# Softmax rows turned on VectorE and put in place by GpSimd, and dense rows as 128 half rows, in a recurrent-memory transformer kernel

## The chip, the cores and the metric

The kernel runs on one core of a Trainium2 chip. The time is the device time of one execution in microseconds. A core has five engines that run their own instruction streams in order and wait for each other by semaphores: TensorE (PE; its weight loads are listed as PEld), VectorE (DVE), ScalarE (ACT), GpSimd (POOL) and SyncE (SP), which issues DMAs.

## The reference

Two layers, each an attention block with a recurrent memory followed by a dense block. The sequence of 2048 rows of 512 is cut into 64 segments of 32 rows; 8 memory rows stand ahead of each segment, and the attention's output for them is the memory of the next segment.

```python
for s in range(n_seg):
    xs = x[:, s * seg_len:(s + 1) * seg_len, :].copy()
    h = jnp.concatenate([mem, xs], axis=1)              # 40 rows
    q = jnp.einsum('btd,dhe->bhte', h, Wq)              # 32 heads of 128
    k = jnp.einsum('btd,dhe->bhte', h, Wk)
    v = jnp.einsum('btd,dhe->bhte', h, Wv)
    scores = jnp.einsum('bhqe,bhke->bhqk', q, k) * scale
    scores = jnp.where(mask[None, None], scores, -1000000000.0)
    p = _softmax(scores, axis=-1)
    o = jnp.einsum('bhqk,bhke->bhqe', p, v)
    o = jnp.einsum('bhte,hed->btd', o, Wo)
    mem = o[:, :M, :].copy()
    outs.append(o[:, M:, :])
...
x = x + _A_ref(_layernorm(x, axis=-1), A_mem0, A_Wq, A_Wk, A_Wv, A_Wo, A_seg_len)
x = x + _B_ref(_layernorm(x, axis=-1), B_w1, B_w2)      # relu(x w1) w2, inner size 1376
x = x + _A_ref(_layernorm(x, axis=-1), ...)
x = x + _B_ref(_layernorm(x, axis=-1), B_w1, B_w2)
```

## The kernel before

The two layers run interleaved: step k works on segment k of the first layer and segment k - 2 of the second, so there are 66 steps, and 62 of them have both. The 40 rows of each layer stand side by side as 80 columns of a transposed tile `HT` (two of them take turns). All weights stay in SBUF.

A step has these parts. `queries_keys` multiplies the weights of four heads with `HT` (16 matmuls of 80 columns) and copies the result from PSUM to `qT` or `kT`. `scores` does one *unit*: the list `UNITS` has three whole units of eight heads and two half units of four. A unit's scores land in one PSUM bank; VectorE adds the mask (L1144), takes the maximum (L1148), subtracts it (L1151); ScalarE takes the exponential (L1155); VectorE sums (L1158), inverts (L1161) and multiplies into the bf16 tile `P` (L1175; GpSimd can do that too). Then TensorE turns `P` with an identity (L726, `work<-ident,P`), and two masked evictions bring the turned rows to `PT`, once for each half of the partitions, so that the other half is zero (L1198 on ScalarE, L1200 on VectorE). `attend` multiplies values by `PT` (L1217) into `OT`, and `project` multiplies `OT` by `Wo` into the bank `st`. Its memory columns go to the next step's `HT`, its other columns to `OX`.

`finish` is the rest of the layers: `OX` is turned by a DMA to `y` (L920), added to `x` (L924), and `dense_layer` normalises the 64 rows (32 of each layer), turns them (`fill<-ident,xr`), multiplies by `w1` and `w2` (L821). The total goes to `Z` (tile `vx`, L940). The first layer's 32 rows of it are normalised again and turned into the next `HT` as the second layer's input; the statistics go through `rstd`, whose two small operations run on GpSimd (L731, L736). GpSimd also narrows the finished rows for the store (L962), carries the first layer's result into `x` (L957), widens the new input rows (L909) and copies rows to `HT` (L998). Values for later segments are made ahead of time in `late_values` and pass through DRAM.

The order on every engine is made while the kernel is built. Each operation is recorded by `plan.op` with the engines it may run on, planned costs, and what it reads and writes. TensorE's operations are sorted by the table `PLACE` (places in a step, one for each operation and phase); the others follow from planned start times, from `AHEAD` and from the window `LOOK`. So a change of an operation moves the order on all engines, and each engine then runs its list strictly in order. `PAIRED` names the groups that run as pairs of half-width matmuls. Tiles come from rings: `es` (the softmax rows in f32) has two buffers, `PT` three, the PSUM `work` ring five banks.

Of the kernel before, what the change touches and what calls it, by code (L numbers as in the profile page):

```python
# [30 lines left out]
LOOK = 0.0763052  # L31
PERIOD = 26.155362
PLACE = {
# [187 lines left out]
def t_dve(n, rate=1):  # L221
    return 0.07 + 1.042e-3 * n / rate


PART, MASKED = {ACT: 0.13, DVE: 0.10}, {ACT: 0.11, DVE: 0.065}
XBAR = 0.5, 0.2, 2.6


# [1147 lines left out]
```

## Time and profile before

| | |
|---|---|
| runs | 1592.23, 1590.45, 1588.74 us; median 1590.45 |
| profiled execution, first to last instruction | 1588.6 us |
| TensorE busy | 1569.5 us, 99% |
| ScalarE busy | 1165.2 us, 73% |
| VectorE busy | 1082.3 us, 68% |
| GpSimd busy | 314.3 us, 20% |
| granted TensorE clock | 0.998 |

The times do not say which of the runs was profiled; the span is 0.14 us under the fastest and 1.85 us under the median. Matmuls are pipelined, and their ends are modelled in the profile: a group's start and the next group's start tell what it occupies. A line such as L726 or L984 is that of a helper with many callers, so the tiles' names tell the groups apart.

### The profile page before, as it was taken

Reading aid. Unit: us, or ns where it says so; the run is one execution under the profiler, and the core shown is the slowest. Engines: PE = TensorE matmul, PEld = TensorE weight load, DVE = VectorE, ACT = ScalarE, POOL = GpSimd, SP = SyncE. Lnnn points to the kernel's source line nnn. Section 1 sums busy time; section 2 is a strip of 40 time slices with the busy share of each in tenths; the row PEclk is TensorE's granted clock in tenths of the full one; section 3 lists DMA queues with packets and bytes.
Section 4 is the critical chain, followed back from the end, with each engine's and each line's share of the span. In section 5 each row is a group of like instructions: output and inputs, shape, how many; then the busy total and the mean of one; then the engine's idle time right before and its main releaser. Section 6 shows DMA issues by size and latency. Waiting matters only on the chain.

```text
span 1588.6 us, 100346 instructions
## 1 busy us (share of the span) xinstructions
PE 1569.5 (99%) x45458; PEld 1411.1 (89%) x45458; DVE 1082.3 (68%) x2957; ACT 1165.2 (73%) x3073; POOL 314.3 (20%) x667
## 2 busy tenths in 40 slices
PE   8999999999999999999999999999999999999998
PEld 5689999999999989999989999999998998898887
DVE  4566766766776776686676677677667667667665
ACT  4667777777777777777777777777777777777774
POOL 5112112212112212121121221211211121112110
PEclk9999999999999999999999999999999999999999
DMA  9711111111111111111111111111111111111100
GB/s 371 243 44 30 26 33 32 29 35 37 25 39 31 35 29 33 29 32 40 26 36 27 35 26 42 37 26 38 25 35 28 33 33 29 33 25 22 28 21 9
DMA packets 76540, 70.89 MB, mean 45 GB/s; under 512 B 50920, under 2 KB 62416, under 8 KB 76112
## 3 DMA queue, kind: packets, MB, share of 16 engines
q1 hardware_dynamic: 70096, 44.14, 13.1%
q0 software_dynamic: 4992, 19.40, 3.4%
q8 instruction: 356, 5.83, 1.6%
q10 hardware_dynamic: 1024, 0.93, 0.2%
q14 instruction: 72, 0.59, 0.1%
HBM read 31.53 MB, written 9.96 MB: 26 GB/s over the span
## 4 chain that ended last, share of the span: by engine, by line
PE 97%; DMA 1%; DVE 1%; POOL 1%; ACT 0%; issue 0%; DVEq 0%; POOLq 0%
PE work L726 40%; PE st L726 19%; PE fill L1048 16%; PE fill L726 8%; PE fill L821 5%; PE work L1217 5%; PE work L1133 4%; DMA xg<-in_A_x_dram 0%; DMA y<-OX 0%; DMA w_sb<-in_B_w_dram 0%; ACT HT L982 0%; POOL Wo_sb L537 0%; PE fill L711 0%; DVE ln L749 0%; POOL ln L736 0%
## 5 line engine op out<-in xcount | busy, mean ns | idle before, releaser
L726 PE MATMUL work<-HT,Wq_sb 128*128 128x80 bf16 (+2 forms) x10400 | 361.8, 201 | 3.1 <-ACT HT L982 3.1
L726 PE MATMUL work<-HT,Wk_sb 128*128 128x80 bf16 (+2 forms) x10416 | 362.7, 201 | 0.8 <-ACT HT L982 0.8
L726 PEld LDWEIGHTS <-Wq_sb 128*128 128x128 bf16 (+1 forms) x10400 | 330.9, 104 | 20.8 <-issue 6.0
L726 PE MATMUL st<-OT,Wo_sb 128*128 128x80 bf16 (+1 forms) x8448 | 345.5, 201 | 0.0
L726 PEld LDWEIGHTS <-Wk_sb 128*128 128x128 bf16 (+1 forms) x10416 | 327.1, 104 | 17.3 <-issue 2.0
L726 PEld LDWEIGHTS <-Wo_sb 128*128 128x128 bf16 x8448 | 315.7, 100 | 13.0 <-issue 12.7
L1048 PE MATMUL fill<-Wv_sb,HT 128*64 128x512 bf16 x2112 | 273.6, 381 | 1.1 <-DVE HT L984 1.0
L982 ACT CAST kT<-work 128x320 bf16<-128x320 f32 (+1 forms) x523 | 218.3, 418 | 68.6 <-PE work L726 31.1
L982 ACT CAST qT<-work 128x320 bf16<-128x320 f32 (+1 forms) x516 | 215.7, 418 | 67.5 <-PE work L726 47.2
L1198 ACT ACTIVATE PT<-work,half 128x160 bf16<-128x160 f32 (+1 forms) x515 | 231.3, 463 | 20.1 <-PE work L726 12.7
L982 ACT CAST OT<-work 128x320 bf16<-128x320 f32 (+1 forms) x461 | 186.2, 420 | 50.7 <-PE work L1217 50.6
L982 ACT CAST vw<-fill 128x512 bf16<-128x512 f32 x229 | 134.1, 586 | 113.3 <-PE fill L1048 109.8
L1144 DVE TENSOR_TENSOR es<-work,maskb 128x320 f32<-128x320 f32 (+2 forms) x330 | 136.2, 413 | 99.7 <-PE work L1133 93.2
L924 DVE TENSOR_TENSOR xg<-xg,y 64x512 f32<-64x512 f32 x65 | 44.2, 680 | 227.2 <-DMA y<-OX 226.6
L731 POOL TENSOR_SCALAR ln<-ln 32x1 f32<-32x1 f32 (+2 forms) x159 | 46.6, 293 | 566.7 <-DVE ln L752 561.0
L1155 ACT ACTIVATE es<-es 128x320 f32<-128x320 f32 (+2 forms) x330 | 136.1, 413 | 24.4 <-DVE es L1151 16.2
L1048 PEld LDWEIGHTS <-HT 128*64 128x64 bf16 x2112 | 98.9, 110 | 57.0 <-DVE HT L984 1.2
L1151 DVE TENSOR_TENSOR es<-es,mx 128x320 f32<-128x320 f32 (+2 forms) x330 | 136.3, 413 | 4.9
L1148 DVE TENSOR_REDUCE mx<-es 128x8 f32<-128x320 f32 (+2 forms) x330 | 133.9, 406 | 5.4
L1158 DVE TENSOR_REDUCE sm<-es 128x8 f32<-128x320 f32 (+2 forms) x330 | 133.4, 404 | 5.1 <-ACT es L1155 2.2
L1175 DVE TENSOR_TENSOR P<-es,sm 128x320 bf16<-128x320 f32 (+1 forms) x269 | 126.9, 472 | 3.3
L1133 PEld LDWEIGHTS <-qT 128*40 128x40 bf16 x4096 | 93.3, 97 | 35.6 <-ACT qT L982 13.6
(96 smaller groups left out, 2164.8 us busy)
## 6 DMA issues: line engine op xcount, KB each, us to landing
V<-vw SPq DMA_DIRECT2D x248, 48.0 KB
V<-vh SPq DMA_DIRECT2D x120, 64.0 KB
Wq_sb<-in_A_Wq_dram POOLq DMA_DIRECT2D x2, 2048.0 KB, 23.2
Wk_sb<-in_A_Wk_dram POOLq DMA_DIRECT2D x2, 2048.0 KB, 28.6
Wo_sb<-in_A_Wo_dram POOLq DMA_DIRECT2D x2, 2048.0 KB, 39.4
vh<-vg SPq DMA_DIRECT2D x32, 128.0 KB
xb<-in_A_x_dram SPq DMA_DIRECT2D x16, 128.0 KB
Wv_sb<-in_A_Wv_dram POOLq DMA_DIRECT2D x1, 2048.0 KB, 13.2
```

Of the source, the lines that this page charges most:

```text
L726: nc.tensor.matmul(out_[u:v, :], lhsT=lhsT[:, u:v], rhs=rhs, start=start, stop=stop, tile_position=(0, u), **more)
L821: nc.tensor.matmul(yp[64 * u:64 * u + 64, 0:256], lhsT=hT[:, fc, :], rhs=w2_sb[:, fc, 256 * u:256 * u + 256], start=(fc == 0), stop=(fc == ...
L982: nc.scalar.copy(out=out_, in_=in_)
L1048: nc.tensor.matmul(vp[64 * b:64 * b + 64, :], lhsT=cols(c4), rhs=Wv_sb[:, c4, n * 512:(n + 1) * 512], start=(c4 == 0), stop=(c4 == NC4 - 1 ...
L1133: nc.tensor.matmul(v[64 * g2:64 * g2 + L, a, i, b, :], lhsT=qT[:, hi, a * L:(a + 1) * L], rhs=kT[:, hi, a * L:(a + 1) * L], start=True, st ...
L1144: nc.vector.tensor_tensor(out=flat(es[:, A]), in0=flat(sp[:, A]), op=ALU.add, in1=maskb[:, a_lo:a_hi, :].unsqueeze(2).to_broadcast([128, n ...
L1148: nc.vector.tensor_reduce(out=mx[:, As], in_=es3(), axis=AX.X, op=ALU.max)
L1151: nc.vector.tensor_tensor(out=es3(), in0=es3(), op=ALU.subtract, in1=mx[:, As].unsqueeze(2).to_broadcast([128, ns * na, L]))
L1155: nc.scalar.activation(out=es[:, A], in_=es[:, A], func=ACTF.Exp, scale=SCALE)
L1158: nc.vector.tensor_reduce(out=sm[:, As], in_=es3(), axis=AX.X, op=ALU.add)
L1175: (nc.gpsimd if eng == POOL else nc.vector).tensor_tensor(out=o, in0=flat(es[:, A]), op=ALU.mult, in1=sm[:, As].rearrange("p (a s) -> p a ...
L1198: nc.scalar.activation(out=o, in_=i, func=ACTF.Copy, scale=half[:, b:b + 1])
```

## The change

The softmax rows are no longer turned by TensorE. The two heads of a pair now lie in neighbouring bf16 elements, so that a pair is one 32-bit element; the two groups of partitions hold the heads of the two halves of a unit. One VectorE transpose of 32x32 blocks of such elements a unit writes to the unit's `es` buffer. As each block is turned in its place only, the blocks are then copied to `PT`: two copies (`stay`) of the blocks that remain on their partitions and four (`shift`) of those that change them, planned on GpSimd or VectorE. `PT` is zeroed once and has 64 columns a pair with gaps; the attention matmuls read every second bf16 of it. `es` has three buffers.

The dense rows become 128 rows of 256: row 64u + t holds two of the four 128-column blocks of row t. The statistics of two halves are swapped across partitions by two small copies and joined by the aggregate. The turns take two matmuls in place of four, the store two DMAs in place of one, and widen and carry two copies in place of one.

Some tiles move into others' space (`ob` and `xe` into `vx`, `none` and `mb0` into `P`). `PLACE`, `PAIRED`, `AHEAD` and `LOOK` have new numbers. By the built program, 1024 turns of 80 columns leave TensorE, 330 block transposes enter VectorE, and of the 1980 copies 1416 stand on GpSimd and 564 on VectorE.

```diff
-LOOK = 0.0763052
+LOOK = 0.08909153
...
-    p_es = ring("es", 2, [128, 8 * L], F32)
-    p_PT = ring("PT", 3, [128, 2, 4, 2, L])
+    p_es = ring("es", 3, [128, 8 * L], F32)
+    p_PT = ring("PT", 3, [128, 4, 2, 128])
...
+    def layernorm_halves(x, keys, quick=False):
...
+        def swap(eng):
+            for u in range(2):
+                copy_on(eng, ln[64 * u:64 * u + 64, 8:14], ln[64 - 64 * u:128 - 64 * u, 0:6])
...
+        plan.op(DVE, t_dve(256), stats, r=keys, w=[ln])
+        plan.op((ACT, DVE), (0.2, 0.2), swap, w=[ln])
+        plan.op(DVE, 0.11, aggr, w=[ln])
+        rstd(ln, R, quick)
+        plan.op(DVE, 0.26, norm, r=[ln, *keys], w=[xn])
...
-        xnT, xn = p_xm.buf(), layernorm(x, keys, slice(0, n), last)
-        turned(xn, n, ident[:, 0:n], [(NC4 * n, lambda: xnT[:, :, :], same, [], [xnT])])
+        xnT, xn = p_xm.buf(), layernorm_halves(x, keys, last)
+        turned(xn, n, ident[:, :], [(NC4 * n, lambda: xnT[:, :, :], same, [], [xnT])], 2)
...
             def carry():
-                nc.gpsimd.tensor_copy(out=x[R1, :], in_=Z[R0, :])
+                for u in range(2):
+                    nc.gpsimd.tensor_copy(out=x[64 * u + SEG:64 * u + 64, :], in_=Z[64 * u:64 * u + SEG, :])
...
         def block():
-            nc.vector.tensor_tensor(out=flat(es[:, A]), in0=flat(sp[:, A]), op=ALU.add,
-                                    in1=maskb[:, a_lo:a_hi, :].unsqueeze(2).to_broadcast([128, na, ns, L]))
+            nc.vector.tensor_tensor(out=ekg(), in0=sp[:, A].rearrange("p (j g k) -> p j k g", k=L, g=2), op=ALU.add,
+                                    in1=maskb[:, mine, :].unsqueeze(3).to_broadcast([128, nx * na, L, 2]))
...
-        plan.op(DVE, t_dve(n), sub, r=[mx], w=[es])
+        plan.op((POOL, DVE), (t_pool(n), t_dve(n)), sub, r=[mx], w=[es])
...
+        pieces = [(a, a + 1) for a in range(a_lo, a_hi)] if nx == 2 else [(a_lo, a_hi)]
...
-        plan.op(PE, nx * na * 0.0358, turn, r=[*[("P", p, b, x) for b in range(2) for x in xs], "ident"], w=[tp, PT],
-                tile=EITHER, count=nx * na)
...
-            copy_op(n, keep, r=[tp, PT, "half"], w=[(PT, b)], more=MASKED)
+        def turn():
+            nc.vector.transpose(out=es[:, 0:64 * nj].rearrange("p (j k) -> p j k", k=64),
+                                in_=P[:, 0:512].bitcast(F32).rearrange("p (j k) -> p j k", k=64)[:, mine, :])
+
+        def turned_pairs():
+            return es[:, 0:64 * nj].rearrange("p (j k) -> p j k", k=64), PT[:, 0:nj, :, :].bitcast(F32)
+
+        def stay(eng):
+            i, o = turned_pairs()
+            for b in range(2):
+                R = slice(64 * b, 64 * b + 64)
+                (nc.gpsimd if eng == POOL else nc.vector).tensor_copy(out=o[R, :, b, :], in_=i[R, :, :])
+
+        def shift(eng):
+            i, o = turned_pairs()
+            for b in range(2):
+                for c in range(2):
+                    R, T = slice(64 * b + 32 * c, 64 * b + 32 * c + 32), slice(64 * b + 32 - 32 * c, 64 * b + 64 - 32 * c)
+                    (nc.gpsimd if eng == POOL else nc.vector).tensor_copy(out=o[R, :, b, 32 - 32 * c:64 - 32 * c],
+                                                                         in_=i[T, :, 32 * c:32 * c + 32])
+
+        plan.op(DVE, 0.19 + 1.042e-3 * 64 * nj, turn, r=[("P", p, b, x) for b in range(2) for x in xs], w=[es])
+        plan.op((POOL, DVE), (2 * t_copy(64 * nj), 2 * t_dve(64 * nj)), stay, r=[es, "PT0"], w=[PT])
+        plan.op((POOL, DVE), (4 * t_copy(32 * nj), 4 * t_dve(32 * nj)), shift, r=[es], w=[PT])
...
                             nc.tensor.matmul(o[u:u + cols, :, a, :], lhsT=V[:, p, e0 + u:e0 + u + cols],
-                                             rhs=PT[:, a, 2 * i + h2, :, :], start=True, stop=True, tile_position=(0, u))
+                                             rhs=PT[:, (a - a_lo) * nx + i, :, :].rearrange("p b (q g) -> p b q g", g=2)[:, :, 0:L, h2],
+                                             start=True, stop=True, tile_position=(0, u))
```

More of the change, by code (lines that the diff above doesn't have):

```diff
@@ new lines @@
+    ("*layernorm.aggr", 1): -2.919, ("*layernorm.stats", 1): 14.406, ("*make_mask", 1): -97.63,
+    ("*prepare_early.load", 1): 2.425, ("*prepare_more.zero_ox", 1): 0.073, ("*prepare_more.zero_w2", 1): 6.609,
+    ("*rstd.power", 1): -10.457, ("*turned.keep", 1): 211883.404, ("*values.mm", 1): 14.109,
+    ("*zero_columns.zero", 1): -101.323, ("attend.ev", 0): -56.0, ("attend.ev", 1): 20.979,
+    ("attend.ev", 2): -153775.429, ("attend.mm", 1): -3.821, ("attend.mm", 2): 10.868, ("bulk.land", 1): 0.799,
@@ new lines @@
+    ("finish.total_out.da", 2): -6.035, ("finish.total_x.da", 0): 38088.478, ("finish.total_x.da", 1): -203599.359,
+    ("finish.turn", 0): 0.667, ("finish.turn", 1): -0.336, ("finish.turn_near", 2): 60.901,
+    ("finish.widen", 0): -1.713, ("get_x", 1): -6.328, ("idle.spins", 1): -0.445, ("idle.spins", 2): -166.134,
+    ("late_values.ev", 0): -0.453, ("late_values.mm", 0): -0.725, ("late_values.put", 0): 44179.455,
+    ("layernorm.aggr", 0): 0.158, ("layernorm.aggr.dl", 0): -0.435, ("layernorm.aggr.dl", 1): -0.608,
@@ new lines @@
+    ("prep_x.cp", 1): 5.544, ("prepare.get_memory", 1): -0.786, ("prepare.keep", 1): 0.796,
+    ("prepare.place", 1): -4.594, ("prepare.turn", 1): -0.641, ("prepare.zero", 1): 205457.087,
+    ("prepare.zero_bank", 1): 10.885, ("prepare.zero_last", 1): 86706.825, ("prepare_late.load", 0): 26.679,
+    ("project.ev", 0): 0.996, ("project.ev", 1): -20.39, ("project.ev", 2): -66497.265, ("project.first", 1): 8.398,
+    ("project.mm", 0): 3.535, ("project.mm", 1): 0.665, ("project.mm", 2): -36163.929, ("project.rows", 0): 2.402,
@@ new lines @@
+    ("scores.top", 1): -2.632, ("scores.top", 2): 18.506, ("scores.total", 0): 72.585, ("scores.total", 1): 0.731,
+    ("scores.total", 2): 7470.862, ("scores.turn", 0): 31675.409, ("scores.turn", 1): 60698.484,
+    ("scores.turn", 2): 42521.632, ("turned.keep", 0): -51540.387, ("turned.keep.da", 0): -34956.614,
+    ("turned.keep.da", 1): -3.41, ("turned.keep.da", 2): -14.838, ("turned.keep.db", 0): -0.181,
+    ("turned.keep.db", 1): 0.006, ("turned.turn", 0): 56413.837, ("turned.turn.da", 2): 0.692,
@@ L199 @@
+    ("turned.turn.db", 0): 21.85, ("turned.turn.db", 1): 15.19, ("values.ev", 2): 0.007, ("values.mm", 0): 2.283,
+    ("values.mm", 2): 113046.287,
 }
@@ L222, in t_dve @@
     return 0.07 + 1.042e-3 * n / rate
-PART, MASKED = {ACT: 0.13, DVE: 0.10}, {ACT: 0.11, DVE: 0.065}
+PART = {ACT: 0.13, DVE: 0.10}
 XBAR = 0.5, 0.2, 2.6
@@ L646, in make_half @@
             nc.vector.memset(half[:], 0.0)
-            for b in range(2):
-                nc.vector.memset(half[64 * b:64 * b + 64, b:b + 1], 1.0)
         def get_memory():
-            nc.scalar.dma_start(out=mb0[0:M, :], in_=A_mem0[0, :, :])
+            nc.scalar.dma_start(out=mb0[0:M, 0:Dm], in_=A_mem0[0, :, :])
         tp = b_fill.buf()
@@ L671, in prepare @@
         plan.available("memory", 5.5)
-        plan.op(DVE, 0.17, zero_none, w=["none", "set"])
+        plan.op(DVE, 0.30, zero_none, w=["none", "set", *[("P", 3, b, x) for b in range(2) for x in range(2)]])
         plan.op(DVE, 0.4, make_half, w=["half", "set"])
@@ L692, in prepare, with zero_last @@
         plan.op(DVE, 0.12, keep, r=[tp], w=["mem0T"])
+        def zero_last():
+            nc.vector.memset(Pt[2][:], 0.0)
+        plan.op(DVE, 0.30, zero_last, w=[mb0, *[("P", 2, b, x) for b in range(2) for x in range(2)]])
         plan.op(DVE, 0.12, place, r=["mem0T"], w=[("HTm", 0)])
@@ L710, in spin @@
         for u in range(2):
-            nc.tensor.matmul(bank[:, 256 * u:256 * u + 256], lhsT=none[:, 0:128], rhs=none[:, :], start=True, stop=True)
+            nc.tensor.matmul(bank[:, 256 * u:256 * u + 256], lhsT=none[:, 0:128], rhs=none[:, 0:256], start=True, stop=True)
     def idle(t, r=()):
@@ L902, in finish @@
         last = k == nsteps - 1
-        x, keys = xg[k % 2], [("x", k % 2, a) for a in range(2)]
+        x, keys = x_of[k % 2], [("x", k % 2, a) for a in range(2)]
         if 0 in act:
@@ L937, in total @@
         def total(to):
-            for u in range(2):
-                cs = slice(256 * u, 256 * u + 256)
-                nc.vector.tensor_tensor(out=to[RB, cs], in0=x[RB, cs], in1=yp[64 * u:64 * u + 64, 0:256], op=ALU.add)
+            nc.vector.tensor_tensor(out=to[:, :], in0=x[:, :], in1=yp[:, 0:256], op=ALU.add)
         def total_x():
@@ L946, in total_out @@
             total(ob)
[L948 removed]
+        t_total = t_dve(256) + PART[DVE]
         if 0 in act:
@@ L1179, in scores @@
-        plan.op((POOL, DVE), (t_pool(n), t_dve(n)), mul, r=[es, sm], w=[("P", p, b, x) for b in range(2) for x in xs])
-        def turn(cols):
-            rhs = ident[:, :].rearrange("p (g q) -> p g q", g=2)[:, :, 0:L]
-            for a in range(a_lo, a_hi):
-                for i, x in enumerate(xs):
-                    z = nx * a + i
-                    c0 = 256 * a + 128 * x
-                    across(cols, tp[:, z * 2 * L:(z + 1) * 2 * L], P[:, c0:c0 + 128], rhs)
-        PT = p_PT.buf()
@@ L1190, in scores @@
[L1190 to L1202 removed]
+            for a0, a1 in pieces:
+                o = P[:, :].rearrange("p (a c) -> p a c", a=2)[:, a0:a1, 128 * xs[0]:128 * (xs[-1] + 1)]
+                o = (o[:, 0, :] if nx == 2 else o).rearrange("p x (k g) -> p x k g" if nx == 1 else "p (x k g) -> p x k g", k=64, g=2)
+                j = slice((a0 - a_lo) * nx, (a1 - a_lo) * nx)
+                (nc.gpsimd if eng == POOL else nc.vector).tensor_tensor(
+                    out=o[:, :, 0:L, :], in0=ekg()[:, j, :, :], op=ALU.mult,
+                    in1=by_head(sm)[:, j, :].unsqueeze(2).to_broadcast([128, nx * (a1 - a0), L, 2]))
@@ new lines, in scores @@
+        plan.op((POOL, DVE), (len(pieces) * t_pool(n / len(pieces)), len(pieces) * t_dve(n / len(pieces))), mul, r=[es, sm],
+                w=[("P", p, b, x) for b in range(2) for x in xs])
+        PT = p_PT.buf()
+        nj = nx * na
+        def turn():
[3 more added lines that the diff above has]
+            return es[:, 0:64 * nj].rearrange("p (j k) -> p j k", k=64), PT[:, 0:nj, :, :].bitcast(F32)
```

227 lines of the change are left out of this document (106 added, 121 removed), and 225 rows, old and new, of tables (PAIRED, PLACE).

## The prediction

> **What bounds the kernel now.** I read the page first (busy shares, chain that ended last), then the stages by windows, then the timeline of one step on TensorE, on GpSimd and on VectorE, and last the groups by form.
>
> ```profile
> PE 1569.5 (99%) x45458; PEld 1411.1 (89%) x45458; DVE 1082.3 (68%) x2957; ACT 1165.2 (73%) x3073; POOL 314.3 (20%) x667
> ...
> PE 97%; DMA 1%; DVE 1%; POOL 1%; ACT 0%; issue 0%; DVEq 0%; POOLq 0%
> ```
> ```profile
> 400.00:700.00 300.00, 300.00 (x8819) 274.56 (x8814) 208.33 (x559) 226.87 (x598) 58.81 (x125) 1.00 0.15 32
> ```
> The columns of the second are window, length, then busy time of PE, PEld, DVE, ACT and POOL. TensorE has no idle time at all in the steady stretch, at the full clock (1.00). So a step lasts as long as its matmuls, and the other engines matter only when a result comes later than its place in TensorE's fixed order. The chain of waits gives the length of a step:
>
> ```profile
> 107.40 4.76 PE work L726 x128
> ...
> 1516.77 4.75 PE work L726 x128
> ```
> This piece, eight query and key groups, opens each step; 60 steps lie between the two, so one takes (1516.77 - 107.40) / 60 = 23.49 us. Now what TensorE spends on turning the softmax rows and the normalised rows in one step (start, length, group; the next group's start gives what a group occupies):
>
> ```profile
> 706.90 0.28 PE L726 MATMUL fill<-ident,xr 128*128 128x64 bf16 x4
> 707.02 0.74 PE L726 MATMUL work<-HT,Wq_sb 128*128 128x80 bf16 x16
> 707.59 0.45 PE L726 MATMUL work<-ident,P 128*128 128x80 bf16 x8
> 707.91 1.09 PE L726 MATMUL fill<-xnM,w_sb 128*128 128x64 bf16 x32
> ...
> 713.83 0.24 PE L726 MATMUL work<-ident,P 128*128 128x80 bf16 x2
> 713.90 0.20 PE L1217 MATMUL work<-PT,V 128*128 128x80 bf16 x1
> ...
> 717.41 0.26 PE L726 MATMUL fill<-ident,xr 128*128 128x32 bf16 x4
> 717.52 0.73 PE L726 MATMUL st<-OT,Wo_sb 128*128 128x80 bf16 x16
> ```
>
> **What the change takes from TensorE.** The three whole units and two half units of a step need 16 turns: 0.32 us for eight (707.59 to 707.91), 0.14 for four pairs of half width (711.82 to 711.96), 0.07 for each half unit; together 0.60. They go. The turn of the dense rows keeps its size (four of 64 columns took 0.12; two of 128 take 2 x 0.055 by the w2 matmuls, where eight half-width ones of 256 columns, four pairs, take 0.44). The turn of the second layer's input falls from 0.11 to about 0.06. So 0.65 us a step: TensorE alone would need 22.84 instead of 23.49. Over 62 steps with both layers that is 40 us, and 2 in the four steps with one layer: 42 us, if nothing comes late.
>
> **What it takes from and gives to ScalarE and VectorE.** ScalarE loses its 515 evictions of turned rows (231.3 us) and gains some 76 evictions from VectorE: it cannot become the bound. VectorE loses 145 such evictions (73 us). The dense rows become 128 rows of 256 instead of 64 or 32 rows of 512, which halves the long part of statistics, norm, add and total (about 110 us less), and about 50 us of other evictions go to ScalarE. It gains 330 block transposes, no row of which exists; 128x320 f32 takes 0.489 and 128x160 0.320, so 0.15 + 1.05 ns an element, 0.42 for 256 and 0.28 for 128 elements, 116 us. The multiply in two pieces adds 186 x (0.64 - 0.49) = 28. The 564 copies left to VectorE, at about 0.2, and 218 swaps of statistics, at 0.16, add 148. Sum about 1140 us, 72% of the span: not the bound by its load.
>
> Two accesses change step: the attention matmuls read every second bf16, and the first add and the two reductions of the softmax read at a step. No row has such a step. The nearest rows read runs of 16 elements: the early turns, with every second run of the identity (64x64, 202 ns a matmul, where contiguous forms take 193 to 202), and the first group's PSUM eviction L984 of 128x256, which takes 0.41, where the plain L811 takes 0.425. So I take them as free, and keep double time for the attention matmuls, 32 x 0.036 = 1.15 us a step, as the other end. A gain is excluded: no fewer columns move.
>
> **What it gives to GpSimd.** Here the trace has rows, and they decide.
>
> ```profile
> L957 POOL COPY xg<-vx 32x512 f32<-32x512 f32 x64 | 39.0, 609 | 12.0 <-DVE vx L940 8.3
> L998 POOL COPY HT<-xnA 128x128 bf16<-128x128 bf16 x63 | 18.4, 292 | 477.2 <-PE work L726 453.4 <-PE fill L1048 23.7
> ```
> ```profile
> 713.78 0.60 POOL L962 CAST ob<-vx 32x512 bf16<-32x512 f32 x1 [0.26 <-POOL P L1175]
> 714.45 0.61 POOL L957 COPY xg<-vx 32x512 f32<-32x512 f32 x1
> 715.14 0.21 POOL L731 TENSOR_SCALAR ln<-ln 32x1 f32<-32x1 f32 x1
> 715.44 0.56 POOL L736 TENSOR_TENSOR ln<-ln,mhalf 32x1 f32<-32x1 f32 x1
> 716.06 0.60 POOL L909 CAST xg<-xb 32x512 f32<-32x512 bf16 x1
> ```
> 512 elements take 0.605 and 128 take 0.292, whatever the type or the partitions: 0.185 + 0.83 ns an element. So 0.40 for 256, 0.29 for 128, 0.24 for 64. The next copy starts 0.06 after the end of the one before it, with no wait of its own (713.78 + 0.60 to 714.45). A whole unit needs two copies of 256 and four of 128: 1.96 busy, 2.3 with the gaps.
>
> In the new order of a steady step the three whole units, the four small copies of one half unit, two copies that widen x, two that carry the layer's result, the one that narrows it, and the power for the second layer's norm stand on GpSimd one behind the other; VectorE does the rest. TensorE's turn of that norm (the place of 717.41 above) waits for the power. The time of that queue, with 0 at the step's first query group:
>
> - Scores of the first unit go out at 4.60; VectorE starts on them 0.49 later (723.23 to 723.72 in the trace), and here 0.3 more behind a small operation, at 5.4.
> - VectorE's order from there to the end of the first transpose holds 14 operations by these rows, the second unit's among them: 6.1 us, less 0.08 overlap at each change, plus 0.2 for the second exponential: it ends at 10.7.
> - GpSimd starts at 10.8: eleven copies of 256 (4.4), twelve of 128 and the one of HT (3.8), four of 64 (0.95), the two of the power (0.24 + 0.56), 9.9 in all; 29 gaps of 0.06, 1.7; it ends at 22.4.
> - Norm with latencies 0.15 + 0.34 + 0.12: TensorE can turn at 23.0.
>
> TensorE itself reaches that place at 22.84 - 1.12 = 21.7, of which 1.12 is what follows in the step (0.09, 0.57 and 0.46). So it stands 1.3 to 1.5 us in every step, and a step takes 24.2 to 24.3. In the trace of before the same norm ended 0.47 us ahead of its turn (716.94 to 717.41) with one copy of 0.6 behind the power: the cover was small, and the new copies are put in front of it. Everything else queued behind the power, HT's next rows, has a step's time.
>
> Against 23.49 that is +0.8 a step, 62 x 0.8 = 50 us. At the ends: 2 us less TensorE work in the four single steps, and about 2 us more latency in each of the last two, where TensorE already idles (24.1 busy of the last 28.6): +2. The profiled span is 1588.6, the fastest listed run 1588.74, the median 1590.45; I add to the median: 1642 us. A tenth of a microsecond a step is worth 6 us here.
>
> **Rivals.**
>
> 1. *The copies run closer and TensorE stays the bound: faster.* For: the two memsets at the start overlapped by 0.05 instead of a gap, and 30 instructions need only 0.05 each to take back 1.5 us. Against: the 61 pairs of L962 and L957 all show the gap, and GpSimd's L909 pair at 36.05 too (1.26 us for two). Without the gaps the wait vanishes; some 0.2 to 0.4 a step may be left at the third scores and at the dense evictions. 1590 - 42 + 12 = 1560, from 1548 to 1580.
>
> 2. *VectorE and GpSimd also hold each other up: slower still.*
> ```profile
> 714.74 0.48 DVE L1175 TENSOR_TENSOR P<-es,sm 128x160 bf16<-128x160 f32 x1
> 716.23 0.71 DVE L755 TENSOR_SCALAR xr<-vx,ln 32x512 bf16<-32x512 f32 x1
> ```
> The first takes 0.32 where GpSimd is idle, the second 0.53. Both ran into a copy, and ended 0.16 and 0.28 after that copy's end, as if their data had begun to flow only then. With 28 copies in 12 us, the subtractions, multiplies, norms and copies of VectorE will often meet one, and copies will meet them. Letting none of the pairs overlap in the sum above moves the end by 0.3 us: 24.5 to 24.6 a step, 1642 + 18 = 1660, up to 1690.
> The Trainium skill, SBUF — State Buffer, section "SBUF: two separate sides", says that VectorE and GpSimd share a pair of ports as an exclusive lock held for the whole instruction, for VectorE operations with two SBUF inputs or in a two-port mode. By that rule the trace agrees for copies (0.48 and 0.71 above), but not for the one-column power: L1151 takes 0.490 beside it and 0.489 alone.
>
> 3. *The stepped reads cost double on TensorE:* 1.15 us a step on the path, 62 x 1.15 = 71, about 1715 with the wait above partly hidden behind it. Nothing in the trace speaks for it.
>
> 4. *No change:* gain and wait cancel at a wait of 0.65 a step.
>
> **Numbers.** Forecast 0.40 (own range 1615 to 1665), rival 1 0.35, rival 2 0.17, rival 3 0.05, rival 4 0.03. About 0.2%, 3 us, is what a measurement can tell from no change. Faster 0.35, same 0.03, slower 0.62. Cases of both signs hold most of the chance, so the range goes from 1553, inside rival 1, to 1680, inside rival 2; about 0.05 lies below and 0.1 above.
>
> **What would show it.** Right: TensorE idles over 1 us once a step, ahead of the two-matmul turn of the normalised rows, released by VectorE's norm, which was released by GpSimd; GpSimd busy without a pause from the first transpose to the power; copies of 0.40 and 0.29. Wrong: copies that follow each other without a gap, TensorE at 99% again and a step of 22.8 to 23.1; or attention matmuls more than 0.036 apart.

## The result, and the profile after

The changed kernel takes 1640.41 us, the median of four runs (1640.27 to 1641.01). Four runs of the kernel before have the median 1589.92. The ratio is 1.0317, with a 95% interval from 1.0302 to 1.0331. The forecast was 1642. The profiled execution spans 1639.3 us.

The page of after, busy times and the chain that ended last:

```profile
PE 1565.1 (95%) x46050; PEld 1388.2 (85%) x46050; DVE 1183.3 (72%) x3938; ACT 1042.4 (64%) x2746; POOL 755.2 (46%) x2177
...
PE 45%; DVE 23%; POOL 20%; issue 6%; ACT 4%; DMA 3%; POOLq 0%; ACTq 0%; DVEq 0%
```

And the steady window that was shown of before:

```profile
400.00:700.00 300.00, 290.82 (x8702) 262.18 (x8701) 220.94 (x727) 195.76 (x515) 139.37 (x402) 1.00 0.12 29
```

TensorE has lost work (1569.5 to 1565.1 us), and yet the run grew: TensorE now stands idle 9 us in 300, at the full clock. VectorE and GpSimd, 1% each of the chain before, hold 43% of it. The length of a step comes from the first matmul of the output projection, in the timeline of TensorE:

```profile
133.78 1.32 PE L728 MATMUL st<-OT,Wo_sb 128*128 128x80 bf16 x32
...
1560.98 1.21 PE L728 MATMUL st<-OT,Wo_sb 128*128 128x80 bf16 x29
```

Between them lie 59 steps, 24.19 us each. The same two places of before are at 124.91 and 1510.89: 23.49 us. So the 50.7 us between the two spans have three parts: 8.9 until the fourth output projection (133.78 - 124.91), 41.2 in the 59 steps (0.70 each), and 0.6 after them.

One step in the timeline of after, whose first query and key group starts at 693.88. GpSimd first, the end of its queue (widen, carry, narrow, then the two small operations of the power):

```profile
713.01 0.83 POOL L939 CAST xg<-xb 32x256 f32<-32x256 bf16 x2
713.89 0.83 POOL L988 COPY xg<-vx 32x256 f32<-32x256 f32 x2
714.78 0.40 POOL L993 CAST vx<-vx 128x256 bf16<-128x256 f32 x1
715.16 0.22 POOL L733 TENSOR_SCALAR ln<-ln 128x1 f32<-128x1 f32 x1
715.46 0.60 POOL L738 TENSOR_TENSOR ln<-ln,mhalf 128x1 f32<-128x1 f32 x1
```

VectorE beside it, the copies of the last half unit and the norm:

```profile
713.97 0.83 DVE L1237 COPY PT<-es 64x128 f32<-64x128 f32 x2
...
715.04 0.78 DVE L1244 COPY PT<-es 32x64 f32<-32x64 f32 x4
716.09 0.41 DVE L782 TENSOR_SCALAR xr<-vx,ln 128x256 bf16<-128x256 f32 x1 [0.27 <-POOL ln L738]
```

And TensorE, at the attention of the last half unit and at the turn of the normalised rows:

```profile
715.88 0.20 PE L1264 MATMUL work<-PT,V 128*128 128x80 bf16 x1 [0.70 <-DVE PT L1244]
...
717.44 0.35 PE L728 MATMUL fill<-ident,xr 128*128 128x64 bf16 x6 [0.68 <-DVE xr L757]
```

GpSimd's queue began at 703.88 and its power ended at 716.06, 10.0 and 22.2 us after the step's start; the forecast had 10.8 and 22.4. The norm waited for the power (0.27 us) and ended at 22.6 instead of 23.0. But TensorE lost 0.70 us a little earlier, at the attention of the last half unit, whose copies to `PT` VectorE finished late. The wait at 717.44 is not that norm's: in this step four matmuls of new input rows are turned together with the two of the norm, and their own norm (L757, out of bf16 rows) waits for a second power. That is so in 3 of the 59 steps; in 38 others the turn waits for L782, the second layer's norm, and in 18 for nothing. The waits of TensorE over the whole run (in total, times, longest):

```profile
PEld L1264 <- issue: 37.9, 66, 1.0
PE work L1264 <- DVE PT L1244: 33.1, 63, 1.1
...
PEld L728 <- DVE xr L782: 16.7, 42, 4.1
PE fill L728 <- DVE xr L782: 8.8, 23, 3.8
```

The first two are the same wait, seen by weight load and matmul. Measured as starts that come later than the usual distance between the same two matmuls, it is 42.0 us between 134 and 1540 us (0.70 a step), and the turn's is 14.8 (0.25), of which the new rows' norm has 2.6.

Sorted by group, each matmul from its start to the next start, a mean step of the two kernels compares so:

| group | before | after |
|---|---|---|
| output projection, with the two waits behind it | 4.65 | 5.63 |
| scores | 0.94 | 1.16 |
| `w1` | 1.28 | 1.45 |
| attention | 1.15 | 1.20 |
| turns of `P` | 0.60 | 0 |
| query and key groups | 9.36 | 9.27 |
| turns of normalised rows | 0.24 | 0.20 |
| values and `w2` | 5.27 | 5.29 |

The waits are 0.98 of the change, scores and `w1` 0.39, the turns that went -0.60; with the rest it is 0.70.

The 0.39 has its own causes, mostly in waits too short for the profile's list; the times of the trace show them. 0.10 is the switch from another group to the scores, which in after stands once behind `w1`, where before it stood behind a query or key group: that group's total fell by as much. 0.13 lies between the scores and the attention of the first units: in 37 of the 59 steps that attention starts 0.04 us after a copy of GpSimd to `PT` has ended, as here (709.17):

```profile
707.83 1.34 POOL L1244 COPY PT<-es 32x128 f32<-32x128 f32 x4
...
709.22 0.23 PE L1264 MATMUL work<-PT,V 128*64 128x80 bf16 x2
```

Most of another 0.07 and 0.06 are scores that start 0.04 us after an eviction of ScalarE into `kT` or `qT`, each in about 20 steps.

The new operations by form (mean ns is the figure after the comma):

```profile
L1244 POOL COPY PT<-es 32x128 f32<-32x128 f32 x740 | 231.5, 313 | 36.1 <-PE work L728 1.2
L1237 POOL COPY PT<-es 64x256 f32<-64x256 f32 x362 | 144.7, 400 | 244.0 <-ACT kT L1015 88.3 <-DVE es L1227 87.4 <-ACT es L1192 29.5
L1237 DVE COPY PT<-es 64x128 f32<-64x128 f32 x244 | 85.8, 352 | 6.0
...
L1244 DVE COPY PT<-es 32x64 f32<-32x64 f32 x288 | 75.1, 261 | 6.0 <-POOL PT L1237 0.8
```

VectorE's copies are the odd ones. Those that meet no instruction of GpSimd (7 and 19 of them) take 219 and 186 ns; the means are 352 and 261.

### The profile page after: what moved, and what is told of

It is laid out like the page before. It is cut to its first block, busy times and chain, and to the rows that moved or that the text cites. A ratio compares the mean times of both kernels' runs of the same rounds, so it can differ in the third digit from the quotient of the medians.

```text
span 1639.3 us, 104125 instructions
## 1 busy us (share of the span) xinstructions
PE 1565.1 (95%) x46050; PEld 1388.2 (85%) x46050; DVE 1183.3 (72%) x3938; ACT 1042.4 (64%) x2746; POOL 755.2 (46%) x2177
## 3 DMA queue, kind: packets, MB, share of 16 engines
q10 hardware_dynamic: 1024, 0.93, 0.2%
## 4 chain that ended last, share of the span: by engine, by line
PE 45%; DVE 23%; POOL 20%; issue 6%; ACT 4%; DMA 3%; POOLq 0%; ACTq 0%; DVEq 0%
PE work L728 25%; PE fill L1081 10%; POOL PT L1244 7%; PE fill L728 4%; PE st L728 3%; DVE P L1216 3%; POOL PT L1237 3%; DVE sm L1195 3%; DVE es L1181 3%; DMA y<-OX 2%; PE work L1167 2%; POOL ln L738 2%; POOL xg L988 2%; POOL xg L939 2%; DVE es L1227 2%
## 5 line engine op out<-in xcount | busy, mean ns | idle before, releaser
L728 PE MATMUL work<-HT,Wk_sb 128*64 128x80 bf16 (+2 forms) x11424 | 374.2, 201 | 4.7 <-ACT HT L1015 3.6
L728 PE MATMUL work<-HT,Wq_sb 128*64 128x80 bf16 (+2 forms) x11424 | 362.8, 201 | 0.6 <-ACT HT L1015 0.6
L728 PEld LDWEIGHTS <-Wq_sb 128*64 128x64 bf16 (+1 forms) x11424 | 335.5, 106 | 27.3 <-issue 2.8
L728 PEld LDWEIGHTS <-Wk_sb 128*64 128x64 bf16 (+1 forms) x11424 | 332.1, 106 | 11.9 <-issue 7.2
L1244 POOL COPY PT<-es 32x128 f32<-32x128 f32 (+1 forms) x1016 | 295.6, 291 | 49.8 <-PE work L728 1.2
L1237 POOL COPY PT<-es 64x256 f32<-64x256 f32 (+2 forms) x400 | 155.6, 389 | 256.1 <-ACT kT L1015 88.3
L733 POOL TENSOR_SCALAR ln<-ln 128x1 f32<-128x1 f32 x159 | 37.3, 235 | 488.9 <-DVE ln L779 385.2
L1181 DVE TENSOR_TENSOR es<-work,maskb 128x320 f32<-128x320 f32 (+2 forms) x330 | 133.8, 406 | 71.9 <-PE work L1167 62.6
L1216 DVE TENSOR_TENSOR P<-es,sm 128x160 bf16<-128x160 f32 (+1 forms) x506 | 175.6, 376 | 2.1
L955 DVE TENSOR_TENSOR xg<-xg,y 128x256 f32<-128x256 f32 x65 | 27.4, 421 | 198.7 <-DMA y<-OX 198.5
L1264 PE MATMUL work<-PT,V 128*64 128x80 bf16 (+1 forms) x1546 | 108.3, 199 | 35.2 <-DVE PT L1244 32.6
```

The costliest lines, as they stand in the source:

```text
L728: nc.tensor.matmul(out_[u:v, :], lhsT=lhsT[:, u:v], rhs=rhs, start=start, stop=stop, tile_position=(0, u), **more)
L733: (nc.vector if quick else nc.gpsimd).tensor_scalar_add(out=ln[R, 7:8], in0=ln[R, 7:8], scalar1=LN_EPS)
L1181: nc.vector.tensor_tensor(out=ekg(), in0=sp[:, A].rearrange("p (j g k) -> p j k g", k=L, g=2), op=ALU.add, in1=maskb[:, mine, :].unsqueeze ...
L1216: (nc.gpsimd if eng == POOL else nc.vector).tensor_tensor(out=o[:, :, 0:L, :], in0=ekg()[:, j, :, :], op=ALU.mult, in1=by_head(sm)[:, j, : ...
L1237: (nc.gpsimd if eng == POOL else nc.vector).tensor_copy(out=o[R, :, b, :], in_=i[R, :, :])
L1244: (nc.gpsimd if eng == POOL else nc.vector).tensor_copy(out=o[R, :, b, 32 - 32 * c:64 - 32 * c], in_=i[T, :, 32 * c:32 * c + 32])
```

## The experiments

Two theories were to be told apart. The first is the forecast's: **the queue** on GpSimd brings the power late. The second is the forecast's second rival: **stalls**, in which VectorE's and GpSimd's copies hold each other up. A third was added after the trace: VectorE's own chain is too long. The table gives all runs; the start is the time of the fourth output projection, and a step is the mean of the 59 that follow it. The last column is worked out from the traces: for each VectorE operation that meets a GpSimd instruction, its time above the median of the same form when it meets none, summed over the run (those that took less count as nothing; x12's sum leaves out 359 operations whose form never runs alone). Each ratio is to runs of the kernel before that were made beside it.

| kernel | median us | ratio to before, 95% | start | step | lost on VectorE |
|---|---|---|---|---|---|
| before | 1589.92 | | 124.9 | 23.49 | 24 |
| after | 1640.41 | 1.0302 to 1.0331 | 133.8 | 24.19 | 101 |
| x1 five copies on ScalarE | 1596.69 | 1.0027 to 1.0061 | 133.4 | 23.47 | 55 |
| x2 half unit's copies on ScalarE | 1653.45 | 1.0383 to 1.0414 | 135.4 | 24.36 | |
| x3 both | 1703.02 | 1.0697 to 1.0729 | 136.2 | 25.14 | |
| x6 dense half rows alone | 1601.51 | 1.0054 to 1.0091 | 124.1 | 23.64 | |
| x7 power ahead of five copies | 1672.23 | 1.0492 to 1.0538 | 136.6 | 24.75 | |
| x8 same queue, no copies in it | 1626.99 | 1.0220 to 1.0254 | 133.1 | 23.98 | 58 |
| x11 power behind the narrow copy | 1621.08 | 1.0180 to 1.0214 | 136.5 | 23.82 | 83 |
| x9 x7 and early dense layer | 1675.87 | 1.0524 to 1.0559 | 136.0 | 24.81 | |
| x10 x1 and early dense layer | 1607.88 | 1.0098 to 1.0128 | 135.4 | 23.62 | |
| x12 planned anew | 1639.56 | 1.0303 to 1.0337 | 131.1 | 24.22 | 70 |
| x13 four copies in ScalarE's gaps | 1591.55 | 1.0003 to 1.0022 | 132.6 | 23.40 | 58 |
| x14 x13 and a busy start | 1592.17 | 1.0004 to 1.0022 | 131.5 | 23.42 | |

### Where the copies stand (x1, x2, x3)

x1 gives the copies that widen, carry and narrow to ScalarE, in their places in the order:

```diff
-                nc.gpsimd.tensor_copy(out=ob[:, :], in_=Z[:, :])
+                nc.scalar.copy(out=ob[:, :], in_=Z[:, :])
```

> The changed kernel with the two widening, two carrying and the narrowing copy on ScalarE (same planned order), so that the power for the second layer's norm stands five copies (about 2.2 us) earlier on GpSimd. GpSimd-queue theory (the wait is at the turn of that norm): the norm is in time, steady step 24.2 to about 22.9 to 23.1, 1565 to 1580 in all. VectorE-chain theory (the wait is at the attention of the last half unit, whose copies VectorE makes; 0.68 us of it a step in the trace after): that wait stays, only the 0.2 to 0.3 us at the turn and part of the start's 9 us go: 1610 to 1625.

x2 gives ScalarE the copies to `PT` that VectorE does:

```diff
-(nc.gpsimd if eng == POOL else nc.vector).tensor_copy(out=o[R, :, b, :], in_=i[R, :, :])
+(nc.gpsimd.tensor_copy if eng == POOL else nc.scalar.copy)(out=o[R, :, b, :], in_=i[R, :, :])
```

> The changed kernel with the copies that VectorE makes (the half units' stay and shift copies) on ScalarE instead. VectorE-chain theory: the attention of the last half unit finds its rows in time, 0.6 to 0.7 us a step less, about 1598. GpSimd-queue theory: the norm's power comes as late as before, the wait only moves from that attention to the turn: 1630 to 1640.

x3 does both.

> Both moves together. If the two queues are all that holds TensorE, it is the bound again: step 22.9 to 23.1, 1550 to 1570, faster than the kernel before. If stepped reads or the new order itself cost time on TensorE, it stays at 1590 or above.

x1 takes back 43.7 of the 50.5 us, nearly all in the steps (42.7; 0.4 at the start), and lies between the two ranges. The waits at the attention and at the turn are gone (5.5 and 0.2 us in all, where after has 42 and 15), so a VectorE chain that is merely too long is refuted; that a step takes 23.47 us, where the theory of the queue had 22.9 to 23.1, is mostly the short waits at scores and `w1`, which are as long as in after. x2 is 13 us slower than the changed kernel and x3 63, outside what either theory gave x2, and far above 1590 in x3: there the attention of the last half unit starts 0.04 us after ScalarE's copies in every step, which are now the late ones. These two tell nothing of the theories. But x1 does not separate queue from stalls, for it removes both. VectorE's own copies got shorter, as the groups of x1 show:

```profile
L1237 DVE COPY PT<-es 64x128 f32<-64x128 f32 x244 | 63.7, 261 | 6.0
L1244 DVE COPY PT<-es 32x64 f32<-32x64 f32 x288 | 53.9, 187 | 6.0 <-POOL PT L1237 0.8
```

### Queue or stalls (x8)

The five copies are replaced by eight one-column additions, which fill nearly the same time on GpSimd; for the narrow copy:

```diff
-                nc.gpsimd.tensor_copy(out=ob[:, :], in_=Z[:, :])
+                nc.gpsimd.tensor_scalar_add(out=warm[:, 0:1], in0=Z[:, 0:1], scalar1=LN_EPS)
+                nc.gpsimd.tensor_scalar_add(out=warm[:, 0:1], in0=warm[:, 0:1], scalar1=LN_EPS)
```

> The changed kernel with the copies that widen, carry and narrow replaced by eight one-column additions on GpSimd in the same places (3, 3 and 2 of about 0.22 us and a gap), so that the queue ahead of the power is as long as before (2.4 us instead of 2.3) but holds no copy; left out are the new input rows, the first layer's carried result and the stored rows. Theory 'queue': VectorE's copies get shorter, but the power comes no earlier, so the wait only moves from the last half unit's attention to the turn of the normalised rows (0.9 to 1.3 us there): 1630 to 1645. Rival 'stalls': the attention's wait goes with the stalls and nothing takes its place: 1590 to 1605.

The waits of TensorE in x8:

```profile
PEld L728 <- DVE xr L782: 42.0, 57, 4.1
...
PE fill L728 <- DVE xr L782: 31.8, 51, 3.9
...
PE work L1266 <- DVE PT L1246: 5.1, 9, 0.9
```

VectorE's copies are about as short as in x1 (261 and 193 ns), the attention's wait fell from 33.1 to 5.1 us, and the turn's rose from 8.8 to 31.8: the wait moved to the place that the forecast had named. The result lies 3 us under the range of the queue and 22 above that of the stalls. So the queue sets the length of the step, and the stalls stood beside its wait and hid it.

Not even the 13.4 us that x8 gained are the stalls'. Worked out from the two traces, the power ends 22.47 us after the step's first group in after and 22.29 in x8 (means of 58 steps), as the additions took 0.16 us less than the copies. The queue is thus 0.18 us shorter and the step 0.21, and in 40 of the 58 steps, taken one by one, the two differences are equal to 0.01 us. At most 0.03 us a step, 2 us in all, is left for the stalls beside these five copies, as long as the queue is this long.

### The order on GpSimd (x7, x11)

x7 puts the power in front of the five copies, by moving them in the finished order:

```diff
-        for o in plan.order():
+        for o in power_first(plan.order()):
```

> The changed kernel with one reordering: on GpSimd the power of the second layer's norm (and the add ahead of it) stands in front of the copies that widen, carry and narrow, which follow it; the stores stay behind the narrow. Nothing leaves GpSimd. Theory 'queue' (the power comes late because of what stands ahead of it): the wait at the turn of the normalised rows, 0.24 us a step, goes (15 us) and the start gains about 2 us from its idle stretch; the wait at the last half unit's attention (0.68 a step) is VectorE's own and stays: 1620 to 1627. Rival 'stalls' (VectorE's copies to PT are held up by the copies that GpSimd runs beside them, 352 and 261 ns where they take 261 and 187 when the five copies are on ScalarE): with the five copies behind the power, VectorE's copies run beside less and both waits go: 1580 to 1600, and the two groups' means fall. If neither holds: 1640.

It is 32 us slower than the changed kernel: both theories missed. The reason lies in SyncE's queue. In after the turning DMA leaves 0.02 us after its rows are in `OX`; in x7 it stands behind the store, which waits for the narrow copy, and behind a load of values that follows the store. After:

```profile
693.72 0.38 ACT L1015 CAST OX<-st 128x256 bf16<-128x256 f32 x1
694.12 1.22 SPq L951 DMA_TRANSPOSE y<-OX  x1
```

x7, in a step of its own:

```profile
581.50 1.37 SPq L1002 DMA_DIRECT2D out_dram<-vx  x2
...
581.94 0.38 ACT L1015 CAST OX<-st 128x256 bf16<-128x256 f32 x1
...
582.98 1.69 SPq L1101 DMA_DIRECT2D V<-vh  x2
584.77 1.23 SPq L951 DMA_TRANSPOSE y<-OX  x1
```

From the end of the eviction to the issue of the turning DMA it takes 0.08 us on average in after and 1.69 in x7. VectorE's add waits for that DMA at the head of the first unit's softmax, and the whole softmax comes later. In TensorE's groups the loss stands at the scores, 0.94 us a step more than in after. x11 therefore leaves the narrow copy ahead of the power.

> As x7_power_ahead, but the narrow copy stays ahead of the power and the stores keep their place, so that SyncE's queue is as in the changed kernel; only the two widening and the two carrying copies go behind the power. In x7_power_ahead the turning DMA of the rows left 1.69 us after its data were ready (0.08 in the changed kernel), behind the stores that waited for the later narrow. If that queue was what made x7_power_ahead slow: well below 1640 here; the power comes 1.8 us earlier, so the wait at the turn goes (0.24 a step), and the wait at the last half unit's attention shrinks by the 0.25 us that the two stay copies no longer lose beside a widening copy: 1605 to 1622. If moving the widening and carrying copies is itself harmful: 1640 to 1670.

1621.08, at the upper end. x11 differs from x7 only in the place of the narrow copy and the stores behind it, so that place is what made x7 slow. The turn's wait fell from 14.8 to 2.0 us, all of it the new rows' norm, and the attention's from 42.0 to 24.2: the stay copies no longer meet a widening copy (265 ns, 352 in after), but the widening and carrying copies now meet VectorE's four shift copies (269 ns). With the queue 1.7 us shorter (its power ends at 20.78 on average) the turn no longer waits for that power, and the stalls count: 24.2 us at the attention, where x1, as short a queue with fewer stalls, has 5.5.

### The dense half rows alone (x6)

The kernel before, with its softmax and its tables, and the dense rows as 128 half rows.

> The kernel before with the dense rows as 128 half rows alone; softmax rows still turned by TensorE, tables of the kernel before. By the prediction's row (0.05 us a step less on TensorE): 1584 to 1589, hardly to be told from no change. If the half rows (swaps, two carries and widens) hurt by themselves: above 1592.

They cost 11 us by themselves. A step is 0.15 longer, and 0.14 of that lies in the output projection (4.79 us a step, 4.65 before), beside the last half unit; scores, `w1` and `w2` take what they took. The profile's list names no release for so small a wait, but the trace tells it: in all 59 steps the turn of the last half unit's `P` starts 0.05 us after VectorE's multiply into `P` has ended, 0.175 us behind the matmul before it, where 0.036 is usual. Ahead of that multiply VectorE has the two swaps of the statistics in the step looked at (from 623.12, 0.51 us for both), which the half rows brought. That without them the wait would go was not tested.

### The start (x9, x10, x14)

In after, TensorE idles from 83.4 to 87.2 us, waiting for the first layer's first normalised rows, and is then slow. In x9 and x10 the dense layer of step 0 comes earlier, by seven numbers such as:

```diff
-    ("turned.turn.da.0", 2): 134.868
+    ("turned.turn.da.0", 2): 133.40
```

> x7_power_ahead and seven numbers of PLACE: the first dense layer's turn, w1 and w2 matmuls (step 0) stand ahead of the output projection of step 1 again, as in the kernel before, where the changed kernel has w2 behind it and TensorE idles 3.8 us at 83 us and then runs at a granted clock of 0.55 for 7 us. If the new order is the cause of the start's 9 us: 6 to 9 us less than x7_power_ahead and a granted clock of 1.00 between 83 and 94 us. If the start's loss has another cause: within 2 us of x7_power_ahead.

> The kernel with widen, carry and narrow on ScalarE (x1) and the same seven numbers of PLACE. It took 1596.7 without them, of which 8.4 us more than the kernel before at the start: 1586 to 1590 if the order of the start is the cause, 1595 to 1598 if not.

Neither gained: x9 is 3.6 us over x7 and x10 11.2 over x1, both above their two ranges. Of the 11.2 only 2.1 lie at the start; 9.1 lie in the later steps, where TensorE's order is that of x1, but the planner made the order on the other engines anew and gave VectorE eight operations of GpSimd's. So the edit did more than was meant. At the start, the step before became 4 us longer, and TensorE stood 4.7 us in the same stretch of x10, now for the turn of the next dense rows. The order of these matmuls alone is not the cause. x14, made on x13 (below), fills the idle stretch:

```diff
+            if o.key == "turned.turn.db.0" and o.step == 0:
+                b = o.new[0][1][0]
+                for _ in range(15):
+                    spin(b.pool.tiles[b.i])
```

> x13_four_copies_in_act_gaps with 30 matmuls on old data (128x256, results not used) in TensorE's idle stretch at 83.8 to 87 us, ahead of the turn of the first layer's first normalised rows. In the changed kernel the clock granted to TensorE fell to 0.55 from 87.2 to 94.2 us after that idle stretch, and sixteen matmuls took 1.05 us instead of 0.57. If the idle stretch is what brings the clock down: granted clock 1.00 in 87 to 94 us, the step that begins at 76.9 us 3 to 4 us shorter, and 1587 to 1589 in all, a little under the kernel before. If the low clock has another cause: within 0.5 us of x13, and the clock falls all the same.

The windows of after (clock in the third column from the right):

```profile
83.40:87.20 3.80, 0.00 (x0) 0.00 (x0) 3.35 (x11) 0.00 (x0) 2.88 (x8) 0.92 0.08 15
87.20:94.20 7.00, 6.61 (x132) 6.36 (x132) 0.84 (x2) 2.62 (x7) 0.40 (x1) 0.55 0.01 2
```

and of x14:

```profile
87.20:94.20 7.00, 6.64 (x196) 6.19 (x197) 2.00 (x6) 4.00 (x11) 0.60 (x2) 1.00 0.01 2
```

The clock stays at 1.00, so it was the idle stretch that brought it down. But the start is only 1.1 us shorter and the run not at all: 1592.17 and 1591.55. The 3 to 4 us of the expectation were taken from the 0.55 of after; in x13 the clock here is 0.76, which leaves 7 x 0.24 = 1.7 us to win. The turn itself came no earlier (87.21, 87.03 in x13), as it waited for VectorE's norm.

What makes the start 6 to 12 us longer in every kernel with the new order is not settled. The windows say where it lies: up to the fourth output projection TensorE is busy for 116.6 us in after and 114.7 in before, and idle for 17.2 and 10.3. Of the 6.9 us more of idle time, 4.3 lie in the step from 76.5 to 109.5. That this step has 27.4 us of work, where before has 21.7, is mostly work from the steps beside it (20.7 and 23.3, where before has 24.5 and 24.8).

### A new plan, and the best place for the copies (x12, x13)

The planner reckons a GpSimd copy at 0.06 us + 1.3 ns an element: 0.39, 0.23 and 0.14 for 256, 128 and 64 elements. With the gap behind them the rows give 0.46, 0.35 and 0.30. x12 has measured costs and a new search of the tables for them:

```diff
 def t_copy(n):
-    return 0.06 + 1.3e-3 * n
+    return 0.245 + 0.83e-3 * n
```

> The instructions of the changed kernel, with the planner's costs set to this case's rows (a copy on GpSimd 0.245 us + 0.83 ns an element with its gap, where the code has 0.06 + 1.3 ns; on VectorE 0.155 + 0.78; a block transpose 0.09 + 1.042 ns an element; the power 0.87; the swap 0.37) and PLACE, AHEAD, PAIRED and LOOK searched anew for these costs; nothing else is changed. The same copies stand on GpSimd or VectorE, wherever the planner puts them. If the loss comes from an order that was made for copies shorter than they are: 1580 to 1600, steady step 23.4 to 23.6. If the copies' own length and the stalls between VectorE and GpSimd make the chain to the last half unit too long in any order: 1605 or more. If it is under 1585, it beats the kernel before.

1639.56, no better than after: the second of the two cases. The plan moved copies to VectorE (820 to `PT`, where after has 564), and VectorE's chain took GpSimd's place; the 70 us and more that VectorE lost beside GpSimd are in no cost of the planner. The chain that ended last:

```profile
DVE 49%; PE 42%; issue 4%; ACT 3%; POOL 1%; DMA 1%; DVEq 0%; POOLq 0%; ACTq 0%; SPq 0%
```

That the costs were too low is so; that a better order would follow from mending them was not shown, nor, by one search, that no order does better. x13 goes back to x1, puts four of its copies where ScalarE has gaps, and gives the narrow copy back to GpSimd:

```diff
+            elif o.key == "attend.evu4.0":
+                out += [(m, 0) for m in widens] + [(o, None)] + [(m, 1) for m in widens]
```

> The changed kernel with the two widening and two carrying copies on ScalarE, but not in their planned places as in x1_five_copies_act: one widening copy ahead of the last attention eviction of the step, one behind it, and the two carrying copies ahead of the next eviction of values, where ScalarE has idle times of 0.4 to 0.8 us in the trace of x1_five_copies_act; the narrow copy stays on GpSimd. In x1_five_copies_act the output projection waited 16.8 us over the run for attention evictions behind these copies, against 9.9 in the changed kernel. Steady step 23.3 to 23.4 instead of 23.47, and the start's 8 us unchanged: 1586 to 1594. If ScalarE's copies cost as much wherever they stand: 1597 or more.

1591.55, as expected, and the best version with the change. It has 5.7 us less in the steps than before (59 x (23.49 - 23.395)), 7.7 more at the start and 1.0 less at the end. No version here beats the kernel before.

## Why the prediction was right

**What bounds it.** TensorE at 23.49 us a step was the bound, and 0.65 us of turns was what could be won. The turns gave what was forecast (0.60 and 0.05). TensorE alone was put at 22.84. Without the two great waits (0.95) and the short ones at scores and attention (0.26) a step of after has 23.0, so that term was nearly right; the shortest steps of x13 take 22.9 to 23.1 us. What the sum lacked is the short waits, on GpSimd's first copies and on ScalarE's evictions. They stay in x13, where the great waits are gone: scores and `w1` are 0.43 over before there.

**The prices.** ScalarE fell from 73% to 64% busy, as forecast no bound. GpSimd's copies were forecast at 0.40, 0.29 and 0.24 us and took 0.400, 0.313 and 0.234. A gap of 0.04 to 0.07 between copies stayed: rival 1, copies that run closer, is out. The block transposes took 0.435 and 0.301 (0.42 and 0.28 forecast), and VectorE's sum was 1183 us against about 1140; the difference is smaller than the 77 us by which its losses beside GpSimd grew by the table's count (24 to 101). The stepped reads are free, as taken: attention matmuls still start 0.036 us apart, and the mask add of 128x320 takes what it took. That puts rival 3 out.

**The queue.** Its end was forecast at 22.4 us of the step and was at 22.2 in the step shown, 22.5 on average; the norm was forecast at 23.0 and ended at 22.6, 22.9 on average. x8 shows the wait that was forecast, at the turn of the normalised rows, as soon as the stalls are out of the way, and x1 shows that without the five copies it is gone. That the queue's end agrees so well is partly luck: it began 0.4 us earlier than was put, and GpSimd was not busy without a pause, as the forecast's sign had it, but stood 0.56 us a step on average, in half of the steps 0.85 until VectorE had turned the second unit.

**What was wrong in it.** First, the place. The text said that TensorE idles over 1 us ahead of the two-matmul turn. It idled 0.70 at the last half unit's attention and 0.25 at the turn. The step that failed is the one that priced VectorE's copies at about 0.2 us and left their meeting with GpSimd to rival 2: the last half unit's two stay copies took 0.41 us instead of 0.22 on average, and its four shift copies 0.26 instead of 0.19, together 0.68 more on the way to the last attention. Rival 2's mechanism was therefore at work, but beside the queue and not on top of it: the rival had 18 us on top of the 50, x8 leaves it 2, and only where the queue is short (x11) does it cost more. Second, the sum. The great waits were put at 1.3 to 1.5 us a step and were 0.95; short waits added 0.26 that was not in it. 62 steps at 0.8 were to give 50 us and the ends 2. The steps gave 41 and the start 9; the total agreed because these errors cancelled. Third, the dense half rows were to take 0.05 us a step from TensorE; alone they cost 11 us in all (x6). That the start could lose as much was not seen: the forecast looked at the new order of steady steps alone.

The Trainium skill, SBUF — State Buffer, section "SBUF: two separate sides", says that VectorE and GpSimd hold a shared pair of ports against each other for an instruction, where VectorE reads two inputs from SBUF or works in a two-port mode. These traces agree in part. VectorE's 64x128 copies take 302 ns beside GpSimd's copies of 128 elements and 404 to 427 beside those of 256, 219 alone; two-input multiplies take 398 and 318, and the reductions lose nothing (478 and 476). But beside GpSimd's one-column operations the copies lose next to nothing (64x128 in x8: 224), as the forecast had seen at the power. In which mode the copies run the traces do not tell.

## What to carry to other kernels

Work that is taken from the bound and given to an idle engine must be laid against that engine's queue in time, not its load: GpSimd was busy 46% of the span, and yet one power late in its queue set the length of the step. Two engines that hold each other up may have to be costed as a pair: a plan with each engine's true cost alone (x12) did no better than one with false costs; that costs for the pair would do better was not tried. A wait that is seen at one place can hide another: when x8 took the longer one away, the other grew in its place. And when an operation is moved past a queue, look for what waits for it on the other queues: x7 lost 32 us because a store stood ahead of another DMA. An experiment that is to leave a queue as long as it was needs its queue measured too.

## What the runs showed of the hardware that was not expected

After 3.8 us without matmuls TensorE's granted clock was 0.55 for about 7 us, and sixteen 80-column matmuls took 1.05 us instead of 0.57; filling the stretch with matmuls kept it at 1.00 (x14). The Trainium skill, TensorE: Matmul & The Clock Gate, Part 1, gives an idle window of about 3.4 us after which the array runs at half rate; the trace agrees. What it costs was tested by x14 against x13 alone, where the clock in this stretch was 0.76: the start got 1.1 us shorter and the run not at all.

The widening and carrying copies on ScalarE (x1) did not overlap: two of 0.41 us took 0.82, while two evictions of 320 columns took 0.75 with 0.43 each. That they stay in SBUF is not enough for it: the narrowing copy does too, and overlapped the eviction behind it by 0.09. Which of their properties it is was not tested.

VectorE's copies are slowed by GpSimd's copies and not by its one-column operations: the 32x64 copies take 388 ns beside a carrying copy in after, and 188 beside the two operations of the power, which is what they take alone (186).
